# Turning the fourth tile of attention weights by DMA, with one normalization for a pair of heads

## The chip, the cores and the metric

The kernel runs on one NeuronCore of a Trainium2 chip. The metric is the device time of one execution in microseconds. TensorE (PE) multiplies into PSUM, VectorE (DVE) and ScalarE (ACT) read PSUM, GpSimd (POOL) works from SBUF alone, and SyncE (SP) issues all the DMAs of the loop. Each engine works its own instructions off in the order in which they were written, and waits on semaphores for the others.

## The reference

The program is a transformer block with adaptive layer norms: attention over the last 512 cached keys, then a gated MLP. The change touches the attention alone.

```python
h = _layernorm(x) * (1 + ca) + sa
q = (h @ wq).reshape(B, Sq, 32, 128).transpose(0, 2, 1, 3)       # Sq = 2048, x has 576 columns
k, v = (repeat(c[:, :, Sk - 512:, :], 2, axis=1) for c in (k_cache, v_cache))  # 16 heads of keys and values, each used twice
p = softmax(einsum("bhqd,bhkd->bhqk", q, k) * 128 ** -0.5)
o = einsum("bhqk,bhkd->bhqd", p, v)
x = x + ga * (o.transpose(0, 2, 1, 3).reshape(B, Sq, 32 * 128) @ wo)
...                                                               # second norm, then the MLP
```

## The kernel before

Nearly every product is made in float16 halves: a float32 operand is split in a high half (a cast) and a low half (the operand less its high half), and three matmuls (high by high, high by low, low by high) stand for one.

The attention is a list of 128 *slots*. A slot `i` is one query head with one block of 512 queries; slots come in pairs, an even slot with head j = 0 and an odd one with j = 1, both of the same key head and the same block. In a slot there are four *steps* t = 0 to 3, one for each tile of 128 queries. The main loop writes the work of one step down for all engines, and that written order is the order on every engine; no scheduler moves anything. Work of several slots is interleaved. In slot `i`:

- Step t: `scores(i, t)` makes the 128x512 scores (three matmuls into a bank `pss`, L400), DVE finds the row's maximum (L404) and turns it into the exponent's bias (L405), and `weights(i, t)` is the exponential on ACT with the row's sum beside it (L417, into `p` and column t of `l`).
- Tiles 0, 1 and 2: ACT casts `p` to its high half (`half_high`, L449), POOL makes the low half (`half_low`, L454), and two steps later SP issues a transposing DMA of both halves (`turn_away`, L461) into `ptw`, the weights with the keys on the partitions. The buffers `hp` that hold both halves are four (HF = 4).
- Tile 3: one slot on, at step 1, PE turns the float32 tile with four transposes into a bank of its own (`turn`, L440, a pool "T" of two banks), ACT casts it into `ptw` (`turn_high`, L444), DVE makes the low half (`turn_low`, L469, step 2).
- Steps 0 to 2: `query(i + 1, t)` makes the queries of the next slot in a bank `pq`; ACT copies the high half out at step 2 (L384), and `query_low(i + 1)` on DVE makes the low half at step 3 (L390).
- At the slot's end `values(i - 1)` multiplies `ptw` by the values: 12 matmuls into a bank `po` (L479). `pq` and `po` take turns in the two banks of the tag "A".
- `sums`: DVE inverts the row sums of slot i - 1 (L424), SP writes the 128x4 numbers to memory (`row`, L427) and reads them back spread over all partitions (`r`, L430, 256 KB). `normalize(i - 2)` at step 1 multiplies `po` by `r` (DVE, L488), and `split_on(i - 2)` at step 3 makes both halves `o` of the result (ACT L498, POOL L499).
- `attend_out`: each step has six matmuls of 288 columns (L353) that multiply `o` of an earlier pair by `wo`, into one bank pair `pe`, and after the second head DVE adds the result, times a factor, to the residual `acc` (L507).

Between these the loop holds side work in fixed places (weights of the MLP are split and stored, L679 to L738; keys and values are prepared). The MLP follows from slot 127 on.

## Time and profile before

| | us |
|---|---|
| median of three runs (2784.73 to 2787.59) | 2786.5 |
| the profiled execution | 2786.65 |
| its span, first to last instruction | 2784.8 |
| PE busy | 2707.0 (97%) |
| DVE busy | 2002.7 (72%) |
| POOL busy | 1864.4 (67%) |
| ACT busy | 1624.1 (58%) |

The span is the time between the first and the last instruction; what lies around it is 1.85 us here. Busy times are means over stages that differ: the attention ends near 1600 us, and DMA engines and POOL are far busier before that point than behind it. The matmuls' ends are modelled, so that successive matmuls overlap in the rows by some 0.16 us; the distance between two starts is the better measure of what a matmul takes.

### The profile page before, as it was taken

The numbers are of one execution on the slowest core, as the hardware profiler recorded it, in microseconds if no ns is written. First come the engines' busy times: TensorE is split into PE (matmuls) and PEld (weight loads), VectorE is DVE, ScalarE is ACT, GpSimd is POOL, SyncE is SP. The second block draws the span as 40 slices with busy tenths as digits, with TensorE's granted clock in tenths as the row PEclk, the third lists the DMA queues.
The fourth block names the chain that finished last, engine by engine and source line by source line (L and its number), as shares of the span: only waits on it lengthen the run. The fifth ranks groups of instructions, "written<-read, shape, count | busy, mean of one in ns | idle before, by whom it ended". The sixth has DMA issues, their size and how long they took to land.

```text
span 2784.8 us, 45011 instructions
## 1 busy us (share of the span) xinstructions
PE 2707.0 (97%) x15536; PEld 1535.3 (55%) x15536; DVE 2002.7 (72%) x3556; ACT 1624.1 (58%) x3022; POOL 1864.4 (67%) x1729
## 2 busy tenths in 40 slices
PE   6999999999999999999999999999999999999998
PEld 3455555555555555555555555555555555555555
DVE  7776788777788787887876657777766656566566
ACT  4686777777777877777677635544443333333332
POOL 3567788888788877777669637688774455333435
PEclk9999999999999999999999999999999999999999
DMA  5777888877777888878879945656643444333332
GB/s 162 177 168 187 189 186 185 179 178 187 169 181 172 187 200 186 212 181 205 194 185 220 233 125 169 195 165 199 206 152 103 160 123 127 104 102 112 105 110 77
DMA packets 594421, 463.27 MB, mean 166 GB/s; under 512 B 443152, under 2 KB 472976, under 8 KB 593424
## 3 DMA queue, kind: packets, MB, share of 16 engines
q1 hardware_dynamic: 593584, 460.39, 64.4%
q8 instruction: 122, 2.00, 0.3%
q14 instruction: 107, 0.88, 0.1%
q10 hardware_dynamic: 608, 0.00, 0.0%
HBM read 263.60 MB, written 95.99 MB: 129 GB/s over the span
## 4 chain that ended last, share of the span: by engine, by line
PE 50%; DVE 3%; DMA 1%; POOL 1%; issue 1%; ACT 0%; SPq 0%; DVEq 0%; POOLq 0%; ACTq 0%
PE py L764 15%; PE px L764 11%; PE pe L849 7%; PE pf L849 6%; PE pe L353 3%; PE po L479 2%; PE pss L400 2%; PE pq L342 2%; DMA row<-l 1%; DMA r<-row 0%; PE pt L440 0%; DVE acc L507 0%; DVE table L404 0%; PE pq L346 0%; POOL hp L454 0%
## 5 line engine op out<-in xcount | busy, mean ns | idle before, releaser
L454 POOL TENSOR_TENSOR hp<-p,hp 128x512 f16<-128x512 f32 x384 | 447.9, 1169 | 285.3 <-ACT hp L449 161.9
L417 ACT ACTIVATE p<-pss,table,factors 128x512 f32<-128x512 f32 x512 | 396.9, 775 | 362.0 <-DVE table L405 183.9
L764 PEld LDWEIGHTS <-wset 128*128 128x128 f16 x3528 | 345.7, 98 | 336.7 <-issue 4.0
L404 DVE TENSOR_REDUCE table<-pss 128x1 f32<-128x512 f32 x512 | 350.5, 685 | 211.8 <-PE pss L400 210.7
L764 PE MATMUL py<-hset,wset 128*128 128x512 f16 x2016 | 483.6, 380 | 0.0
L353 PE MATMUL pe<-o 128*128 128x288 f16 x3072 | 458.8, 286 | 14.6 <-DVE acc L507 12.5
L400 PE MATMUL pss<-k,qT 128*128 128x512 f16 x1536 | 417.3, 380 | 11.2 <-ACT p L417 9.2
L353 PEld LDWEIGHTS <-o 128*128 128x128 f16 x3072 | 300.4, 98 | 187.8 <-issue 20.9
L479 PE MATMUL po<-ptw,v 128*128 128x512 f16 x1536 | 358.2, 381 | 7.4 <-DVE ptw L469 5.6
L764 PE MATMUL px<-hset,wset 128*128 128x512 f16 x1512 | 361.5, 379 | 1.6 <-ACT p L417 1.6
L342 PE MATMUL pq<-hT,wq 128*128 128x512 f16 x1092 | 281.3, 380 | 1.1 <-DVE hT L211 1.1
L91 POOL TENSOR_TENSOR akv<-u,akv 128x512 f16<-128x512 f32 x141 | 164.8, 1178 | 174.6 <-ACT akv L90 166.8
L449 ACT CAST hp<-p 128x512 f16<-128x512 f32 x384 | 237.3, 618 | 12.9 <-POOL hT L213 0.4
L479 PEld LDWEIGHTS <-v 128*128 128x128 f16 x1536 | 150.9, 100 | 169.6 <-issue 16.8
L849 PEld LDWEIGHTS <-akv 128*128 128x128 f16 x1728 | 169.6, 98 | 93.6 <-issue 4.5
L400 PEld LDWEIGHTS <-qT 128*128 128x128 f16 x1536 | 150.4, 100 | 123.5 <-issue 12.6
L507 DVE SCALAR_TENSOR_TENSOR acc<-pe,factors,acc 128x576 f32<-128x576 f32 x256 | 207.7, 812 | 13.7 <-PE pe L353 10.4
L499 POOL TENSOR_TENSOR o<-on,o 128x512 f16<-128x512 f32 x128 | 150.2, 1173 | 55.8 <-ACT o L498 52.4
L342 PEld LDWEIGHTS <-wq 128*128 128x128 f16 x1104 | 108.6, 98 | 138.4 <-issue 9.0
L843 DVE SCALAR_TENSOR_TENSOR acc<-pf,table,acc 128x576 f32<-128x576 f32 x140 | 113.5, 811 | 80.6 <-PE pf L849 80.6
L944 ACT COPY u<-py 128x512 f32<-128x512 f32 x72 | 42.2, 586 | 200.5 <-PE py L764 198.6
L937 ACT ACTIVATE s<-s,table 128x512 f32<-128x512 f32 x72 | 52.0, 722 | 173.0 <-DVE s L936 173.0
(228 smaller groups left out, 4826.4 us busy)
## 6 DMA issues: line engine op xcount, KB each, us to landing
wset<-wd SPq DMA_DIRECT2D x213, 320.0 KB, 3.2
r<-row SPq DMA_DIRECT2D x128, 256.0 KB, 4.0
oset<-od SPq DMA_DIRECT2D x106, 288.0 KB, 3.2
wraw<-in_w SPq DMA_DIRECT2D x36, 768.0 KB, 5.5
wd<-wmade SPq DMA_DIRECT2D x75, 320.0 KB, 3.2
wset<-wd SPq DMA_DIRECT2D x71, 160.0 KB, 2.2
w2raw<-in_w SPq DMA_DIRECT2D x19, 576.0 KB, 4.9
wd<-ring SPq DMA_DIRECT2D x33, 320.0 KB, 2.8
```

Source lines behind the costliest of these rows:

```text
L91: eng.tensor_sub(halves[:, 1], src, halves[:, 0])
L342: nc.tensor.matmul(ps, w[:, k // 2, m, :], hT[:, DC + m if k == 1 else m, :], start=s == 0, stop=False)
L353: nc.tensor.matmul(E[:, h, :HALF], o[:, x, rows], w[:, y, h * HALF : (h + 1) * HALF], start=first and n == 0, stop=last and n == 2,)
L400: nc.tensor.matmul(pss, q[:, x, rows], k[:, y, :], start=n == 0, stop=n == 2)
L404: nc.vector.tensor_reduce(nm[:, 0:1], pss, axis=AX.X, op=ALU.max, negate=True)
L417: nc.scalar.activation(p, pss, AF.Exp, bias=nm[:, 1:2], scale=factor, accum_out=st["l"][:, t : t + 1])
L449: nc.scalar.copy(hp[:, 0, :], state[i]["p", t])
L454: nc.gpsimd.tensor_sub(hp[:, 1, :], state[i].pop(("p", t)), hp[:, 0, :])
L479: nc.tensor.matmul(po, v[:, x, c, :], pt[:, y, c, :], start=c == 0 and n == 0, stop=c == KC - 1 and n == 2)
L507: nc.vector.scalar_tensor_tensor(a, E[:, :, :HALF], factors[:, uses[u][0], 2:3], a, op0=ALU.mult, op1=ALU.add)
L764: nc.tensor.matmul(ps, w[:, a, :], h[:, b, :], start=start and n == 0, stop=stop and n == 6, skip_group_check=True)
L849: nc.tensor.matmul(ps[:, h, :HALF], a[:, rows], w[:, b, :], start=m == 0, stop=m == 2)
```

## The change

- All four tiles are split in SBUF (`half_high`, `half_low`) and turned by DMA; `turn`, `turn_high` and `turn_low` are gone. `turn_away` of tiles 2 and 3 stands at steps 0 and 1 of the following slot.
- The two "T" banks, which PE's transposes used, take the scores of tiles 0 and 2, so that scores have four banks.
- The even slot's head is not normalized. `normalize` and `split_on` bring `po` times 2^-24 straight into its halves: the high half on ACT at step 1, the low half on DVE at step 3, which reads `po` once more. The odd slot's head is multiplied by the ratio of both sums, and the inverse of the first head's sum goes into the factor with which `attend_out` adds to the residual. The sums of a pair lie in one tile `l`, and `sums` inverts, writes `row` and reads `r` once for a pair.

In the order of the instructions this shows at three places. All are from slot 60 (an even one) on; the names of tiles carry running numbers, and the line numbers differ a little between the programs (L404 is L405 in the changed one, L390 is L391, L479 is L468, L461 is L455).

PE at the end of slot 60, before: the last matmuls of `attend_out`, a small matmul of side work, then `values(59)`.

```order
L353 LDWEIGHTS o_8939
L353 MATMUL pe_76<-o_8802,o_8939 128x288
L1077 MATMUL pe_76<-table_217,ones_93 128x1 [waits DVE_49]
L479 LDWEIGHTS v_8356 [waits DMAHW5_49,DMAHW3_49,DMAHW1_49]
L479 MATMUL po_9103<-ptw_8893,v_8356 128x512 [waits Activation_49]
L479 LDWEIGHTS v_8356
L479 MATMUL po_9103<-ptw_8893,v_8356 128x512
L479 LDWEIGHTS v_8356
L479 MATMUL po_9103<-ptw_8893,v_8356 128x512 [waits DVE_49]
```

The same place now:

```order
L354 LDWEIGHTS o_8585
L354 MATMUL pe_76<-o_8456,o_8585 128x288
L1081 MATMUL pe_76<-table_217,ones_93 128x1 [waits DVE_49]
L468 LDWEIGHTS v_8024 [waits DMAHW3_49,DMAHW5_49,DMAHW2_49,DMAHW0_49]
L468 MATMUL po_8745<-ptw_8538,v_8024 128x512 [waits DVE_49]
L468 LDWEIGHTS v_8024
L468 MATMUL po_8745<-ptw_8538,v_8024 128x512
```

The first matmul of `values` waited for an ACT count and the third for the low half on DVE of the tile that PE had turned; now the group waits for four DMAs and, at its first matmul, for a count of DVE. In the built program that count is the one of `query_low` (L391, below): the tile `po` takes the bank of "A" that was given back first, and that is now the one of `pq`, since the even slot's `po` is read until step 3. This holds in 63 slots, all the even ones from 2 to 126; in the odd ones `po` takes the bank that `normalize` gave back at step 1, as before.

DVE in slot 60, from step 1 to step 3, before:

```order
L488 TENSOR_TENSOR on_9012<-po_8958,r_8927 128x512 [waits DMAHW0_49,Pool_49]
L507 SCALAR_TENSOR_TENSOR acc3_90<-pe_76,factors_95,acc3_90 128x576 [waits PE_49]
L241 TENSOR_REDUCE us_8952<-kvraw_8846 128x1 [waits DMAHW1_49]
L1072 TENSOR_REDUCE table_217<-w2raw_8925 128x1 [waits DMAHW7_49]
L404 TENSOR_REDUCE table_217<-pss_9040 128x1 [waits PE_49]
L405 TENSOR_SCALAR table_217<-table_217,factors_95 128x1 [waits DVE_49]
L469 TENSOR_TENSOR ptw_8893<-pt_9001,ptw_8893 128x4x128 [waits DMAHW3_49,Activation_49]
L404 TENSOR_REDUCE table_217<-pss_9071 128x1 [waits PE_49]
L405 TENSOR_SCALAR table_217<-table_217,factors_95 128x1 [waits DVE_49]
L390 SCALAR_TENSOR_TENSOR qT_9056<-pq_8985,qT_9056 128x512 [waits Activation_49]
L507 SCALAR_TENSOR_TENSOR acc0_87<-pe_76,factors_95,acc0_87 128x576 [waits PE_49]
```

And now:

```order
L511 SCALAR_TENSOR_TENSOR acc3_90<-pe_76,l_7800,acc3_90 128x576 [waits PE_49]
L242 TENSOR_REDUCE us_8598<-kvraw_8498 128x1 [waits DMAHW1_49]
L1076 TENSOR_REDUCE table_217<-w2raw_8569 128x1 [waits DMAHW7_49]
L405 TENSOR_REDUCE table_217<-pt_8682 128x1 [waits PE_49]
L406 TENSOR_SCALAR table_217<-table_217,factors_95 128x1 [waits DVE_49]
L405 TENSOR_REDUCE table_217<-pss_8712 128x1 [waits PE_49]
L406 TENSOR_SCALAR table_217<-table_217,factors_95 128x1 [waits DVE_49,Activation_49]
L391 SCALAR_TENSOR_TENSOR qT_8697<-pq_8632,qT_8697 128x512 [waits Activation_49]
L494 SCALAR_TENSOR_TENSOR o_8655<-po_8604,o_8655 128x512
L511 SCALAR_TENSOR_TENSOR acc0_87<-pe_76,l_8084,acc0_87 128x576 [waits PE_49]
```

`normalize` (L488) and `turn_low` (L469) have gone from the even slot; behind `query_low` stands the low half of the unnormalized head (L494), and `query_low` has kept its place behind the fourth maximum.

SP around the turns of slot 60, before:

```order
L461 DMA_TRANSPOSE ptw_9038<-hp_8981 128x8x128 [waits DMAHW6_49,PE_49,Pool_49]
L430 DMA r_9068<-row59_9020 128x512 [waits DMAHW7_49,DMAHW4_49]
L461 DMA_TRANSPOSE ptw_9038<-hp_9016 128x8x128 [waits DMAHW0_49,Pool_49]
L636 DMA wd14_118<-wmade_8997 128x640 [waits DMAHW1_49]
L461 DMA_TRANSPOSE ptw_9038<-hp_9049 128x8x128 [waits DMAHW2_49,Pool_49]
L427 DMA row60_9162<-l_8978 128x4 [waits DMAHW3_49,DVE_49]
L461 DMA_TRANSPOSE ptw_9182<-hp_9126 128x8x128 [waits PE_49,Pool_49]
```

And now:

```order
L455 DMA_TRANSPOSE ptw_8680<-hp_8627 128x8x128 [waits DMAHW6_49,PE_49,Pool_49]
L436 DMA r_8709<-row59_8662 128x512 [waits DMAHW7_49,DMAHW4_49]
L455 DMA_TRANSPOSE ptw_8680<-hp_8659 128x8x128 [waits DMAHW0_49,Pool_49]
L640 DMA wd14_118<-wmade_8644 128x640 [waits DMAHW1_49]
L455 DMA_TRANSPOSE ptw_8680<-hp_8690 128x8x128 [waits DMAHW2_49,Pool_49]
L455 DMA_TRANSPOSE ptw_8680<-hp_8721 128x8x128 [waits DMAHW3_49,Pool_49]
L455 DMA_TRANSPOSE ptw_8815<-hp_8767 128x8x128 [waits PE_49,Pool_49]
```

A slot has four transposes in place of three, and the even slot has no `row`; the odd one keeps `row` and `r`.

The diff (the removed functions and the main loop):

```diff
@ scores
-        pss = bank("S", "pss")
+        pss = bank("S", "pss") if t % 2 else t_bank()
@ weights
-            st["l"] = odd.tile([P, 2 * ST], F32, tag="l", name="l", bufs=3)
+            st["l"] = odd.tile([P, 6 * ST], F32, tag="l", name="l", bufs=4) if j == 0 else state[i - 1]["l"]
...
-        nc.scalar.activation(p, pss, AF.Exp, bias=nm[:, 1:2], scale=factor, accum_out=st["l"][:, t : t + 1])
+        nc.scalar.activation(p, pss, AF.Exp, bias=nm[:, 1:2], scale=factor, accum_out=st["l"][:, j * ST + t : j * ST + t + 1])
@ sums
+        if j == 0:
+            return
+        first, both, up, ratio = (st["l"][:, lo * ST : hi * ST] for lo, hi in ((0, 1), (0, 2), (2, 4), (4, 5)))
         if step == 0:
-            nc.vector.reciprocal(st["l"][:, ST:], st["l"][:, :ST])
+            nc.vector.reciprocal(up, both)
+            nc.vector.scalar_tensor_tensor(ratio, first, O_DOWN, up[:, ST:], op0=ALU.mult, op1=ALU.mult)
@ turn, turn_high, turn_low
-        for j in range(KC):
-            nc.tensor.transpose(ps[:, j, :], p[:, j * P : (j + 1) * P], ident)
-        nc.scalar.copy(st["pt"][:, 0, :, t * P : (t + 1) * P], st["t"])
-    nc.vector.tensor_sub(pt[:, 1, :, cols], state[i]["t"], pt[:, 0, :, cols])
@ normalize
+        if slots[i][1] == 0:
+            o = st["o"] = new_o(i)
+            nc.scalar.activation(o[:, 0, :], st["po"], AF.Copy, scale=O_DOWN)
+            return
@ split_on
+        if slots[i][1] == 0:
+            o, po = st["o"], st.pop("po")
+            nc.vector.scalar_tensor_tensor(o[:, 1, :], po, O_DOWN, o[:, 0, :], op0=ALU.mult, op1=ALU.subtract)
+            return
         on = st.pop("on")
+        nc.vector.tensor_scalar(
+            st["l"][:, 5 * ST :], st["l"][:, 2 * ST : 3 * ST], factors[:, uses[slots[i][0]][0], 2:3], 1.0 / O_DOWN,
+            op0=ALU.mult, op1=ALU.mult,
+        )
@ attend_out
-                a, E[:, :, :HALF], factors[:, uses[u][0], 2:3], a, op0=ALU.mult, op1=ALU.add
+                a, E[:, :, :HALF], state[2 * pair]["l"][:, 5 * ST + t : 5 * ST + t + 1], a, op0=ALU.mult, op1=ALU.add
@ main loop
-            if t == 0 and 1 <= i <= n:
-                turn_away(i - 1, 2)
-            slot, tile = (i - 1 if t == 1 else n, ST - 1)
-            if 0 <= slot < n:
-                turn(slot, tile)
+            if t < 2 and 1 <= i <= n:
+                turn_away(i - 1, t + 2)
...
-            if 1 <= i <= n and t == 2:
-                turn_low(i - 1, ST - 1)
...
-            if t < 3 and i < n:
+            if i < n:
                 half_high(i, t)
                 half_low(i, t)
-            if t == 1 and 1 <= i <= n:
-                turn_high(i - 1, ST - 1)
```

More of the change, by code (lines that the diff above doesn't have):

```diff
@@ L42 @@
 Q_DOWN = 2.0**-17
+O_DOWN = 2.0**-24
 EXPONENT = 0x7F800000
@@ L414, in weights @@
         if t == 0:
-            st["l"] = odd.tile([P, 2 * ST], F32, tag="l", name="l", bufs=3)
+            st["l"] = odd.tile([P, 6 * ST], F32, tag="l", name="l", bufs=4) if j == 0 else state[i - 1]["l"]
         p = pool.tile([P, SB], F32, tag="p", name="p", bufs=PB)
-        nc.scalar.activation(p, pss, AF.Exp, bias=nm[:, 1:2], scale=factor, accum_out=st["l"][:, t : t + 1])
+        nc.scalar.activation(p, pss, AF.Exp, bias=nm[:, 1:2], scale=factor, accum_out=st["l"][:, j * ST + t : j * ST + t + 1])
         st["p", t] = p
     def sums(i, step):
+        u, j, b = slots[i]
         st = state[i]
+        if j == 0:
+            return
+        first, both, up, ratio = (st["l"][:, lo * ST : hi * ST] for lo, hi in ((0, 1), (0, 2), (2, 4), (4, 5)))
         if step == 0:
-            nc.vector.reciprocal(st["l"][:, ST:], st["l"][:, :ST])
+            nc.vector.reciprocal(up, both)
+            nc.vector.scalar_tensor_tensor(ratio, first, O_DOWN, up[:, ST:], op0=ALU.mult, op1=ALU.mult)
         elif step == 1:
             st["row"] = dram.tile([P, ST], F32, name=f"row{i}")
-            nc.sync.dma_start(st["row"], st["l"][:, ST:])
+            nc.sync.dma_start(st["row"], ratio)
         elif step == 2:
@@ L432, in sums @@
             )
-    def turn(i, t):
-        st = state[i]
-        p = st.pop(("p", t))
-        ps = st["t"] = t_bank().rearrange("p (j n) -> p j n", j=KC)
-        for j in range(KC):
-            nc.tensor.transpose(ps[:, j, :], p[:, j * P : (j + 1) * P], ident)
-    def turn_high(i, t):
-        st = state[i]
-        nc.scalar.copy(st["pt"][:, 0, :, t * P : (t + 1) * P], st["t"])
     def half_high(i, t):
@@ L464, in turn_away @@
         )
-    def turn_low(i, t):
-        cols = slice(t * P, (t + 1) * P)
-        pt = state[i]["pt"]
-        nc.vector.tensor_sub(pt[:, 1, :, cols], state[i]["t"], pt[:, 0, :, cols])
     def values(i):
@@ L482, in values, with new_o @@
         st["po"] = po
+    def new_o(i):
+        return pool.tile([P, 2, SB], F16, tag=("ah", "al")[i % 2], name="o", bufs=3)
     def normalize(i):
         st = state[i]
+        if slots[i][1] == 0:
+            o = st["o"] = new_o(i)
+            nc.scalar.activation(o[:, 0, :], st["po"], AF.Copy, scale=O_DOWN)
+            return
         po = st.pop("po")
@@ L495, in split_on @@
         st = state[i]
+        if slots[i][1] == 0:
+            o, po = st["o"], st.pop("po")
+            nc.vector.scalar_tensor_tensor(o[:, 1, :], po, O_DOWN, o[:, 0, :], op0=ALU.mult, op1=ALU.subtract)
+            return
         on = st.pop("on")
-        o = st["o"] = pool.tile([P, 2, SB], F16, tag=("ah", "al")[i % 2], name="o", bufs=3)
+        nc.vector.tensor_scalar(
+            st["l"][:, 5 * ST :], st["l"][:, 2 * ST : 3 * ST], factors[:, uses[slots[i][0]][0], 2:3], 1.0 / O_DOWN,
+            op0=ALU.mult, op1=ALU.mult,
+        )
+        o = st["o"] = new_o(i)
         nc.scalar.copy(o[:, 0, :], on)
```

## The prediction

> **What bounds the kernel now.** I read the shares of the page first, then the busy times of stretches of the span, then what PE waited for.

> ```profile
> PE 2707.0 (97%) x15536; PEld 1535.3 (55%) x15536; DVE 2002.7 (72%) x3556; ACT 1624.1 (58%) x3022; POOL 1864.4 (67%) x1729
> ```

> ```profile
> core 0: us, PE busy (x) PEld busy (x) DVE busy (x) ACT busy (x) POOL busy (x), PEclk, DMA share, GB/s
> 250.20:1017.30 767.10, 756.15 (x4353) 427.88 (x4352) 605.10 (x1210) 596.13 (x1154) 649.24 (x627) 1.00 0.79 182
> 1017.30:1476.80 459.50, 455.78 (x2653) 260.66 (x2652) 359.56 (x734) 341.08 (x664) 332.31 (x308) 1.00 0.84 197
> 2000.00:2100.00 100.00, 96.55 (x542) 53.65 (x541) 69.44 (x98) 42.18 (x72) 70.54 (x63) 0.97 0.47 154
> ```

> The first two stretches are 64 and 38 slots of the attention, about 12 us each; PE is busy for 98.6% and 99.2% of them. The third lies in the MLP, which the change leaves alone. What PE waits for in the attention (45 to 1600 us):

> ```profile
> PE pss L400 <- ACT p L417: 9.2, 10, 2.5
> PE pe L353 <- DVE acc L507: 7.6, 10, 1.7
> PE po L479 <- DVE ptw L469: 5.6, 8, 2.9
> PE po L479 <- DMA ptw<-hp: 1.0, 2, 0.6
> ```

> All its waits there come to some 36 us. So PE is the bound: a matmul removed is a gain of its full length, and any wait put in front of PE is a loss of its full length.

> **What the change removes from PE.** The four transposes of a slot, in slot 60:

> ```profile
> 780.44 0.60 PE L440 MATMUL pt<-ident,p 128*128 128x128 f32 x4
> 780.88 0.81 PE L400 MATMUL pss<-k,qT 128*128 128x512 f16 x3
> ```

> From start to start they take 0.44 us; 128 slots give **-56 us**. Of the waits above, that for `turn_low` (5.6) goes with it; that for a bank of scores (9.2) should go with four banks; and that for `acc` (7.6) should halve, since DVE loses work. I take **-19 us**, between 0 (new lateness elsewhere) and -36 (all of them).

> **What the change puts in front of PE.** In the 63 even slots the first matmul of `values` now waits for `query_low` on DVE. The trace has no such wait, but it has both times. The end of slot 60:

> ```profile
> 785.59 0.81 PE L400 MATMUL pss<-k,qT 128*128 128x512 f16 x3
> 786.17 0.67 DVE L404 TENSOR_REDUCE table<-pss 128x1 f32<-128x512 f32 x1
> 786.24 0.90 PE L353 MATMUL pe<-o 128*128 128x288 f16 x6
> 787.11 2.95 PE L479 MATMUL po<-ptw,v 128*128 128x512 f16 x12
> 787.60 0.68 DVE L404 TENSOR_REDUCE table<-pss 128x1 f32<-128x512 f32 x1
> 788.32 0.21 DVE L405 TENSOR_SCALAR table<-table,factors 128x1 f32<-128x1 f32 x1
> 788.61 0.59 ACT L384 ACTIVATE qT<-pq 128x512 f16<-128x512 f32 x1
> 789.23 0.69 DVE L390 SCALAR_TENSOR_TENSOR qT<-pq,qT 128x512 f16<-128x512 f32 x1 [0.70 <-ACT qT L384]
> 789.89 0.81 PE L400 MATMUL pss<-k,qT 128*128 128x512 f16 x3
> ```

> `values` starts at 787.11 and `query_low` ends at 789.92, 2.81 us later. Before, that was hidden: only the third matmul of the next scores needed it, and the 2.6 us of `values` lay between. Now `values` itself stands behind it, and PE has nothing else to do. The same pair of rows in the first of the 63 slots, in the one with the least distance, and in the last:

> ```profile
> 80.88 0.59 PE L479 MATMUL po<-ptw,v 128*128 128x512 f16 x2
> 83.57 0.69 DVE L390 SCALAR_TENSOR_TENSOR qT<-pq,qT 128x512 f16<-128x512 f32 x1 [0.70 <-ACT qT L384]
> 354.94 2.76 PE L479 MATMUL po<-ptw,v 128*128 128x512 f16 x12 [0.25 <-ACT qT L384]
> 354.96 0.69 DVE L390 SCALAR_TENSOR_TENSOR qT<-pq,qT 128x512 f16<-128x512 f32 x1
> 1583.94 2.75 PE L479 MATMUL po<-ptw,v 128*128 128x512 f16 x12
> 1584.36 0.69 DVE L390 SCALAR_TENSOR_TENSOR qT<-pq,qT 128x512 f16<-128x512 f32 x1
> ```

> The distances are 3.38, 0.71 and 1.11; over the 63 slots the mean is 1.87, and 0.06 for the signal comes on top. So the upper end, if DVE and ACT are as late as now, is 63 x 1.93 = 122 us. The lower end is a slot in which neither is late: the slot at 354.94 had already waited 0.25, so it stands for 0.71 + 0.25 + 0.06, about 1.0 us, and 63 us in all. Lateness shrinks in part, because the even slot's DVE loses `normalize` and `turn_low`:

> ```profile
> L488 DVE TENSOR_TENSOR on<-po,r 128x512 f32<-128x512 f32 x128 | 138.9, 1085 | 16.8 <-POOL o L499 8.4 <-DMA r<-row 6.1 <-PE po L479 1.8
> L469 DVE TENSOR_TENSOR ptw<-pt,ptw 128x512 f16<-128x512 f32 x128 | 87.6, 684 | 26.6 <-ACT ptw L444 25.5 <-DMA row<-l 0.4 <-issue 0.2
> DVE qT L390 <- ACT qT L384: 62.2, 82, 1.8
> ```

> The last row (DVE's waits, 70 to 1600 us) says that in 82 of 126 slots DVE stood waiting for ACT's copy, so it is mostly ACT that is late there. But ACT's copy follows the exponential of tile 2, which waits for DVE's third maximum, and that one stood behind L488. In slot 60 it began at 786.17, about 2 us after its scores; without L488 all of this comes 1.07 us earlier. In a slot such as the last, nothing is gained. I take half a microsecond on average: 1.4 us a slot, **+88 us**.

> **What moves between the other engines.**

> ```profile
> L454 POOL TENSOR_TENSOR hp<-p,hp 128x512 f16<-128x512 f32 x384 | 447.9, 1169 | 285.3 <-ACT hp L449 161.9 <-issue 79.3 <-DVE table L405 16.8
> L449 ACT CAST hp<-p 128x512 f16<-128x512 f32 x384 | 237.3, 618 | 12.9 <-POOL hT L213 0.4
> L444 ACT CAST ptw<-pt 128x512 f16<-128x512 f32 x128 | 74.1, 579 | 0.6 <-PE pt L440 0.6
> L498 ACT CAST o<-on 128x512 f16<-128x512 f32 x128 | 78.1, 610 | 7.1 <-DVE on L488 7.1
> L499 POOL TENSOR_TENSOR o<-on,o 128x512 f16<-128x512 f32 x128 | 150.2, 1173 | 55.8 <-ACT o L498 52.4
> L461 SPq DMA_TRANSPOSE ptw<-hp x384: 1231/1239/3839, 45.1 to 1602.2; - x192
> DMA to landing us min/median/max: 3.0/3.8/8.2
> r<-row SPq DMA_DIRECT2D x128, 256.0 KB, 4.0
> SPq L461 <- POOL hp L454: 201.9, 101, 7.4
> ```

> ACT: 128 casts at 0.618 for 128 at 0.579, and 64 copies of `o` at 0.6 taken from PSUM instead of SBUF: +5 us in 1500, nothing. DVE: -128 x 0.684, -64 x (1.085 - 0.69), some 0.2 us rows less and more: about -110 us, which PE sees only as above. POOL: +128 x 1.169 - 64 x 1.173 = +75 us, 0.58 us a slot; it is busy 649 of 767 us in the fuller stretch, 10.1 us a slot, and goes to 10.7 of about 12.2, 88%. SP: one more issue of 1.24 us a slot, and half of the `row` and `r` issues gone. DMA engines: a transpose moves 256 KB, as `r` does. Its price is bounded by 1.1 us of all engines (their 606 busy microseconds in that stretch by 139 MB) and by 1.8 (the shortest landing, 3.0, less the issue of 1.24); with half an `r` gone that is +0.55 to +1.25 us a slot, and the share goes from 0.79 to 0.84 to 0.89.

> None of these becomes the bound, but two chains get shorter slack. Tile 3 needs a cast, POOL and a transpose before `values` one slot later: 0.62 + 1.17 + 3.8 = 5.6 us without queues. From the exponential's end to `values` there are 9.4 in slot 60 (the row below), less 0.44, plus the new wait of 1.4. And with four tiles a slot in four `hp` buffers, ACT's cast of a tile waits until the same tile of the slot before has landed: 5.6 us plus queues against a whole slot of 12. SP already waits up to 7.4 us for POOL, so some turns will be late: I take one slot in eight by 1 us, **+15 us**, between 0 and one in four by 2 us, 64.

> ```profile
> 776.90 0.78 ACT L417 ACTIVATE p<-pss,table,factors 128x512 f32<-128x512 f32 x1
> ```

> [...]

> **Sum.** -56 - 19 + 88 + 15 = +28 us. The profiled execution took 2786.65 us (0.15 above the median of the runs shown), so 2815 us.

> **Rivals.**
> - *Faster: DVE comes early enough.* The point of balance is a new wait of (56 + 19 - 15) / 63 = 0.95 us a slot. At the lower end of 1.0 us, with no new lateness and all of PE's old waits gone, it is 2786.65 - 56 - 36 + 63 = 2758. For it: DVE loses 110 us. Against: 82 waits of DVE for ACT, whose work stays.
> - *The wait doesn't exist* (`values` still goes ahead of `query_low`): 2786.65 - 56 - 19 + 15 = 2727. Against it stands the order of the instructions.
> - *POOL or the DMA engines fall behind,* so that turns are late as a rule: the upper ends of both, +122 + 64 - 56 - 19, 2898. For it: POOL at 88%, DMA at 0.89. Against: PE's 1.0 us.
> - *The clock drops.* The row of 2000 to 2100 us shows 0.97, and PE waited once there, for 3.4 us; a wait of 2.9 us in the attention left the clock at 1.00. The 0.03 of 100 us that are missing there are 3 us, a clock halved for 6. If the new waits were over 3 us in every even slot (their mean is 1.87, the first one 3.38), 63 x 3 = 189 us come on top, 3004.

> ```profile
> PE pe L849 <- DVE sums L843: 3.4, 1, 3.4
> ```

> [...]

> **How the numbers follow.** The forecast, slower by 0 to 85 us, has 0.66; faster by an early DVE 0.17; no wait 0.03; POOL or DMA 0.12; the clock 0.02. A difference under 0.2% (5.6 us) can't be told from none. Between the forecast's lower edge and the first rival's upper one lies that band, 0.09 in all: 0.05 from the forecast and 0.04 from the rival. So slower 0.61 + 0.12 + 0.02 = 0.75, same 0.09, faster 0.13 + 0.03 = 0.16. The range goes from the lower end of the first rival, 2758, to 2878 (the upper new wait of 122 with 45 of lateness, less 56 and 19); below and above it lie the no-wait case, half of POOL's and the clock's, and the tails, under 2 in 10.

> **What would show it.** PE's waits after should name `po` and DVE's `qT` (L391) 60 times or so, 60 to 120 us in all, about 1.4 us each, and no longer `ptw` from DVE. The distance of the scores' first matmul from the last matmul before it at step 1 shrinks by 0.44 us. Waits of PE for `ptw` from DMA should stay under 20 us, and waits of ACT's `hp` cast for a DMA be few. Even slots get longer by about 1 us, odd ones shorter by 0.5. The prediction is wrong if DVE's `qT` ends less than 0.9 us behind PE's arrival, or if `po` waits longer for DMAs than for DVE.

## The result, and the profile after

The changed kernel takes 2916.6 us (four runs, 2916.5 to 2916.9) against 2785.8 for the kernel before on the same chip (the three runs shown above and a fourth): 4.7% slower, ratio 1.0469 with a 95% interval of 1.0451 to 1.0487. The forecast was 2815, between 2758 and 2878. The direction was right; the size was not, and the time lies outside the range.

The engines' busy times, the two stretches that the prediction used, and PE's waits in the attention (45 to 1740 us; in total, times, longest):

```profile
PE 2704.9 (93%) x15024; PEld 1490.5 (51%) x15024; DVE 1964.0 (67%) x3492; ACT 1639.3 (56%) x3022; POOL 1936.6 (66%) x1793
```

```profile
core 0: us, PE busy (x) PEld busy (x) DVE busy (x) ACT busy (x) POOL busy (x), PEclk, DMA share, GB/s
250.20:1017.30 767.10, 696.22 (x3764) 373.44 (x3764) 538.33 (x1081) 549.73 (x1051) 621.91 (x599) 0.96 0.78 177
1017.30:1476.80 459.50, 416.67 (x2278) 224.91 (x2277) 325.90 (x664) 328.16 (x631) 352.37 (x323) 0.97 0.82 190
```

```profile
PE po L468 <- DVE qT L391: 128.2, 60, 5.5
PE po L468 <- DMA row<-l: 10.2, 2, 6.0
PE po L468 <- DMA ptw<-hp: 8.5, 3, 4.4
PE pe L354 <- DVE acc L511: 2.2, 2, 1.3
```

PE was busy for 98.6% of the first stretch before and is busy for 90.8% of it now, and its clock, 1.00 before, is 0.96. The wait that the prediction named is there, in 60 of its 63 slots, but at 2.14 us each and not 1.4. The end of slot 60, which the prediction showed for the kernel before:

```profile
846.82 0.81 PE L401 MATMUL pt<-k,qT 128*128 128x512 f16 x3
847.02 0.82 DVE L511 SCALAR_TENSOR_TENSOR acc<-pe,l,acc 128x576 f32<-128x576 f32 x1 [0.87 <-PE pe L354]
849.07 0.81 PE L401 MATMUL pss<-k,qT 128*128 128x512 f16 x3
849.61 0.68 DVE L405 TENSOR_REDUCE table<-pt 128x1 f32<-128x512 f32 x1
850.45 0.28 PE L1081 MATMUL pe<-table,ones 128*128 128x1 f32 x2
852.06 0.59 ACT L385 ACTIVATE qT<-pq 128x512 f16<-128x512 f32 x1
852.68 0.69 DVE L391 SCALAR_TENSOR_TENSOR qT<-pq,qT 128x512 f16<-128x512 f32 x1 [1.22 <-ACT qT L385]
853.43 4.41 PE L468 MATMUL po<-ptw,v 128*128 128x512 f16 x12 [2.70 <-DVE qT L391]
857.67 0.81 PE L401 MATMUL pt<-k,qT 128*128 128x512 f16 x3
```

PE ends its small matmul at 850.73 and stands until 853.43. Then the twelve matmuls of `values` take 4.41 us, where the row of before had 2.95: PE's clock is halved. The same moments by windows of 3.41 us, with the granted clock in the third column from the right:

```profile
846.57:849.98 3.41, 3.41 (x23) 1.98 (x21) 2.96 (x4) 2.00 (x4) 2.28 (x4) 1.00 1.19 221
849.99:853.40 3.41, 0.74 (x8) 0.60 (x6) 2.04 (x6) 2.73 (x6) 1.16 (x1) 1.00 1.09 187
853.41:856.81 3.40, 3.38 (x9) 1.14 (x9) 2.45 (x7) 2.95 (x6) 3.18 (x4) 0.50 0.43 87
```

One wait is paid twice: 2.70 us of standing, and some 1.5 us of slow matmuls behind it.

### The profile page after: what moved, and what is told of

Its sections match the earlier page's. It is cut to its first block, busy times and chain, and to the rows that moved or that the text cites. A ratio compares the mean times of both kernels' runs of the same rounds, so it can differ in the third digit from the quotient of the medians.

```text
span 2914.7 us, 44120 instructions
## 1 busy us (share of the span) xinstructions
PE 2704.9 (93%) x15024; PEld 1490.5 (51%) x15024; DVE 1964.0 (67%) x3492; ACT 1639.3 (56%) x3022; POOL 1936.6 (66%) x1793
## 3 DMA queue, kind: packets, MB, share of 16 engines
q8 instruction: 118, 1.93, 0.3%
## 4 chain that ended last, share of the span: by engine, by line
PE 51%; DVE 5%; ACT 3%; issue 2%; POOL 1%; DMA 1%; SPq 0%; ACTq 0%; DVEq 0%; POOLq 0%
PE py L768 15%; PE px L768 11%; PE pe L853 6%; PE pf L853 6%; PE po L468 4%; PE pe L354 3%; PE pq L343 2%; PE pt L401 1%; PE pss L401 1%; DVE table L405 1%; ACT p L418 1%; ACT hp L443 1%; DVE acc L511 1%; DVE qT L391 1%; ACT qT L385 0%
## 5 line engine op out<-in xcount | busy, mean ns | idle before, releaser
L448 POOL TENSOR_TENSOR hp<-p,hp 128x512 f16<-128x512 f32 x512 | 598.3, 1172 | 387.8 <-ACT hp L443 218.0
L468 PE MATMUL po<-ptw,v 128*128 128x512 f16 x1536 | 402.0, 417 | 151.4 <-DVE qT L391 128.2
L418 ACT ACTIVATE p<-pt,table,factors 128x512 f32<-128x512 f32 x256 | 198.5, 775 | 416.5 <-DVE table L406 374.1
L468 PEld LDWEIGHTS <-v 128*128 128x128 f16 x1536 | 161.6, 107 | 352.1 <-issue 208.0
L443 ACT CAST hp<-p 128x512 f16<-128x512 f32 x512 | 316.3, 618 | 26.4 <-DMA ptw<-hp 9.4
L405 DVE TENSOR_REDUCE table<-pss 128x1 f32<-128x512 f32 x256 | 176.0, 688 | 180.4 <-PE pss L401 180.2
L405 DVE TENSOR_REDUCE table<-pt 128x1 f32<-128x512 f32 x256 | 174.6, 682 | 156.3 <-PE pt L401 156.2
L511 DVE SCALAR_TENSOR_TENSOR acc<-pe,l,acc 128x576 f32<-128x576 f32 x256 | 207.7, 811 | 43.9 <-PE pe L354 35.3
L418 ACT ACTIVATE p<-pss,table,factors 128x512 f32<-128x512 f32 x256 | 197.8, 773 | 47.3 <-DVE table L406 45.3
L401 PE MATMUL pt<-k,qT 128*128 128x512 f16 x768 | 212.1, 385 | 6.4 <-ACT qT L385 4.3
L401 PE MATMUL pss<-k,qT 128*128 128x512 f16 x768 | 208.9, 381 | 0.0
## 6 DMA issues: line engine op xcount, KB each, us to landing
r<-row SPq DMA_DIRECT2D x64, 256.0 KB, 4.1
```

The source lines that it names most:

```text
L401: nc.tensor.matmul(pss, q[:, x, rows], k[:, y, :], start=n == 0, stop=n == 2)
L405: nc.vector.tensor_reduce(nm[:, 0:1], pss, axis=AX.X, op=ALU.max, negate=True)
L418: nc.scalar.activation(p, pss, AF.Exp, bias=nm[:, 1:2], scale=factor, accum_out=st["l"][:, j * ST + t : j * ST + t + 1])
L443: nc.scalar.copy(hp[:, 0, :], state[i]["p", t])
L448: nc.gpsimd.tensor_sub(hp[:, 1, :], state[i].pop(("p", t)), hp[:, 0, :])
L468: nc.tensor.matmul(po, v[:, x, c, :], pt[:, y, c, :], start=c == 0 and n == 0, stop=c == KC - 1 and n == 2)
```

## Accounts of every kernel

For each profiled execution I added up from its trace, over the attention (first matmul of the scores to the last of `values`): its length, PE's idle time between matmuls (gaps over 0.05 us), and the length of the stretches with a halved clock. A stretch at half clock costs half its length (within one group of 512-column matmuls, a start follows the one before it by a median of 0.427 us in the halved stretches of the changed kernel's trace and 0.216 outside them), and the removed transposes are worth 56 us. So the length should be 1582.2 (before) + change in idle time + half the change in halved time - 56 where the transposes are gone. Halved stretches are counted where they begin in the attention. The rows come from several chips, on which the kernel before took 2785.8 to 2788.6 us; each ratio is to the kernel before on the same chip, and differences of a few microseconds between rows mean little.

| kernel | time, us | ratio to before (95%) | attention | idle | halved | by the sum |
|---|---|---|---|---|---|---|
| before | 2785.8 | | 1582 | 43 | 10 | |
| changed | 2916.6 | 1.0469 (1.0451-1.0487) | 1713 | 174 | 133 | 1719 |
| 1 early split | 2813.0 | 1.0089 (1.0073-1.0106) | 1610 | 108 | 38 | 1605 |
| 2 pair's normalization alone | 2921.5 | 1.0481 (1.0464-1.0499) | 1712 | 147 | 58 | 1711 |
| 3 DMA turns alone | 2857.7 | 1.0251 (1.0235-1.0266) | 1658 | 144 | 61 | 1654 |
| 4 filled wait | 2891.0 | 1.0371 (1.0355-1.0388) | 1693 | 112 | 68 | 1692 |
| 5 early split, two score banks | 2810.8 | 1.0091 (1.0076-1.0106) | 1609 | 103 | 44 | 1604 |
| 6 early split, DVE half | 2807.4 | 1.0080 (1.0059-1.0100) | 1607 | 101 | 55 | 1607 |
| 7 DMA turns alone, DVE half | 2845.0 | 1.0212 (1.0197-1.0227) | 1644 | 129 | 68 | 1642 |
| 8 normalization alone, early split | 2804.0 | 1.0066 (1.0051-1.0081) | 1601 | 58 | 14 | 1600 |
| 9 early split, column parts | 2785.6 | 0.9994 (0.9984-1.0003) | 1579 | 81 | 17 | 1569 |
| 10 normalization alone, copied | 2840.1 | 1.0190 (1.0175-1.0206) | 1638 | 80 | 24 | 1626 |
| 11 changed, copied, column parts | 2895.1 | 1.0390 (1.0374-1.0405) | 1690 | 162 | 68 | 1675 |
| 12 as 8, more POOL work | 2821.0 | 1.0125 (1.0108-1.0142) | 1616 | 70 | 17 | 1613 |
| 13 changed, product's own bank | 2813.2 | 1.0094 (1.0077-1.0112) | 1611 | 105 | 48 | 1607 |
| 14 as 13, column parts | 2788.3 | 1.0003 (0.9994-1.0013) | 1587 | 86 | 27 | 1578 |
| 15 as 14, DVE half | 2789.9 | 1.0012 (1.0002-1.0021) | 1591 | 84 | 31 | 1578 |
| 16 DMA turns alone, own bank, column parts | 2839.3 | 1.0190 (1.0175-1.0206) | 1636 | 122 | 51 | 1627 |
| 17 as 14, a third score bank | 2816.9 | 1.0115 (1.0102-1.0129) | 1614 | 105 | 48 | 1607 |
| 18 as 17, DVE half | 2809.7 | 1.0090 (1.0076-1.0104) | 1609 | 97 | 51 | 1601 |

(In kernel 4 the added matmuls, 315 of some 0.215 us, are counted in.) The account closes within 6 us for the changed kernel and for ten of the others. The seven with column parts lie 7 to 15 us above it; they issue twelve more matmuls a slot, and in their traces the group of `values` takes 2.62 us from its start to the next matmul's, 2.59 in one part, which is 4 us of it. Kernel 10 lies 12 above; 8 us of that are matmuls of the query projection that take longer from start to start, and why stays open. So nearly all of what these edits did to the time is PE's idle time and the clock that follows it, with the 56 us of the transposes as forecast (in the trace of before all 512 of them take 55.9 us, from start to next start).

## The experiments

My theory (A) was the prediction's mechanism, larger: the even slot's product `po` takes the PSUM bank of `pq`, and so `values` waits for `query_low`. The rivals: the clock does most of the harm; the DMA turns themselves are late; POOL is behind.

**1. Release the bank a step earlier.**

```diff
-            if 2 <= i <= n and t == 3:
+            if 2 <= i <= n and t == (3 if slots[i - 2][1] else 2):
                 split_on(i - 2)
```

> The changed kernel with one line moved: the even head's low half (split_on on DVE) stands at step 2 instead of step 3, so that its bank of po is given back before that of pq, and values in the even slots no longer stands behind query_low. Theory A (the loss is the new wait of values for query_low, and the clock that drops behind it): PE's waits for po from DVE's qT, 128 us in the changed kernel, go to under 15 us, the TensorE clock over the attention is back at 0.99 or more, and the time is 2786 - 56 (the turns) - 5 to 20, that is 2710 to 2740 us. Rival B (turning four tiles by DMA overloads POOL and the DMA engines, and the wait for qT is only where it shows): the wait moves to ptw from DMA or to hp, and the time stays over 2850 us.

2813.0 us: 104 us of the 131 are gone, but not all, and the gain that A expected did not come. What PE waits for now:

```profile
PE po L468 <- DMA ptw<-hp: 42.7, 28, 4.7
PE po L468 <- issue: 10.9, 5, 3.0
PE po L468 <- DVE qT L391: 2.2, 1, 2.2
```

The wait for `query_low` has gone from 128.2 us to 2.2. Behind it stood another, for late turns, which it had covered: 35 times `values` waited for a turn, each time for that of tile 3. In those slots its issue ended 7.7 us after the next slot's first scores, in the others 4.7; from the start of the issue to the landing it took 4.3 and 3.8 us. So it is mostly the issue that is late, not the transfer.

**2. The pair's normalization alone** (tile 3 still turned by PE, two score banks, as before).

> The kernel before with the normalization of pairs alone (PE still turns the fourth tile, scores in two banks). Theory A: the order of the release of banks is the same as in the changed kernel, so the 63 waits of values for query_low are there, some 1.9 us each, 120 us in all, and the clock drops behind the longer ones: 2900 to 2970 us. Rival B: nothing is turned by DMA that was not before, so the time is that of before, 2770 to 2800 us.

2921.5 us. As A expected: no DMA turn of tile 3 is needed for the damage.

```profile
PE po L485 <- DVE qT L391: 114.1, 62, 3.1
```

**3. The DMA turns alone** (each head normalized by itself, four tiles by DMA, four score banks).

> The changed kernel without the normalization of pairs: four tiles split in SBUF and turned by DMA, scores in four banks, every head normalized as before (128 r and row transfers, 128 subtractions of o on POOL). Theory A: no wait for query_low, the turns' 56 us are gained: 2710 to 2745 us, though POOL and the DMA engines carry more than in the changed kernel. Rival B: POOL and the DMA engines are the bound, so it is as slow as the changed kernel or slower, over 2880 us.

2857.7 us, between both expectations. A missed: without the wait for `query_low`, turning by DMA still costs 70 us where it should give 56. PE waits in two places, for turns (the row "issue" is a wait for which the trace shows no releaser), and at the output projection for DVE's add; DVE in turn stands at `normalize` for a buffer that POOL releases late (last row, DVE's waits):

```profile
PE pe L354 <- DVE acc L494: 40.4, 26, 3.4
PE po L463 <- DMA ptw<-hp: 25.2, 20, 2.8
PE po L463 <- issue: 20.0, 12, 3.0
DVE on L475 <- POOL o L486: 30.6, 17, 3.7
```

So 2 and 3 don't add: +133 and +69 apart, +131 together. The turns' waits lie in the same place as that for `query_low`, which covers them, and the wait for DVE's add, 40.4 us here, is 2.2 with the pair's normalization.

**4. Fill the wait** with five matmuls of 512 columns that nobody reads, ahead of `values` in even slots of the changed kernel.

> The changed kernel with five more 512-column matmuls (1.08 us, into a free bank of scores, read by nobody) ahead of values in each even slot, in the time in which PE waits for query_low. Clock theory (part of theory A: the gaps halve the clock, 26 times and 116 us in the changed kernel's attention, which costs about half of that): PE's idle time falls by up to 68 us without the wait ending earlier, the clock drops less than 12 times, and the time falls by 25 to 55 us, to 2860 to 2892 us, although PE does more. If the clock costs nothing: the filler is hidden in the wait or adds to it, 2915 to 2940 us.

2891.0 us: more work on PE, and 26 us less time. The halved stretches fall from 133 to 68 us (16 of them, where fewer than 12 were expected), and the clock of the first stretch rises from 0.96 to 0.99. The clock's share is real, and it is a consequence of idle time.

```profile
250.20:1017.30 767.10, 727.42 (x4007) 392.32 (x4007) 551.96 (x1109) 566.15 (x1081) 637.25 (x615) 0.99 0.81 179
```

**5. Two score banks** in kernel 1, in place of four (`pss = bank("S", "pss")` for all tiles).

> The 2813.0-us run's kernel with the scores in two PSUM banks as before, not four. If four banks are what lets scores run ahead of late maxima and weights: over 2840 us. If PE's order, not the banks, sets the scores' start: 2800-2825 us, the same as with four.

2810.8, the same as kernel 1. Four banks weren't needed; two PSUM banks were free for something else, which 13 uses.

**6 and 7. The low half of tile 3 on DVE,** behind the next slot's first maximum, in kernels 1 and 3.

```diff
-        nc.gpsimd.tensor_sub(hp[:, 1, :], state[i].pop(("p", t)), hp[:, 0, :])
+        (nc.vector if t == 3 else nc.gpsimd).tensor_sub(hp[:, 1, :], state[i].pop(("p", t)), hp[:, 0, :])
...
-                half_low(i, t)
+                if t < 3:
+                    half_low(i, t)
+            if 1 <= i <= n and t == 0:
+                half_low(i - 1, 3)
```

> The changed kernel with the first head's low half taken one step earlier (as in the run at 2813.0 us), and with the low half of the fourth tile of weights made by DVE, behind the first maximum of the next slot, instead of by POOL. Theory P (POOL is behind): in the 2813.0-us run the turn of tile 3 was issued on average 4.1 us (even) and 3.9 us (odd) after the next slot's start, up to 10.3 us, while `values` starts without a wait only if it is issued by about 5.4 us; the cast had ended at 0.3 us, so the lateness is POOL's queue. On DVE the half ends at 2 to 3 us in every slot: PE's idle time before `values` falls from 75 us to under 30 us, and the time to 2735-2775 us. Theory D (the transfers themselves: DMA engines at 0.88 busy): the turn still lands late, idle time stays over 55 us, 2795-2820 us. Theory V (DVE pays): 128 more operations of about 0.6 us on DVE push back maxima and query halves, 2820 us or more.

> Turning all four tiles by DMA without the pair's normalization (the 2857.7-us run), with the low half of the fourth tile on DVE instead of POOL. Theory P: PE's idle time before `values` falls from 65 us to under 25, that before the output projection (which waits for DVE's add, and DVE for a buffer that POOL's late subtraction releases) from 47 us to under 20, and the time to 2745-2800 us. Theory D: 2835-2865 us. Theory V: over 2865 us.

2807.4 and 2845.0: 6 us better, which is within the noise (ratios 1.0080 and 1.0089), and 13, where theory P expected at least 38 and 58. P as I had put it (the last tile's own half is what is late) missed. Both times lie where theory D had them, but its reason, slow transfers, is the smaller part: where `values` waits for tile 3's turn, the issue ends 2.6 and 2.7 us later than in the other slots, and the landing takes 1.0 us longer. Kernel 7 in slot 23 shows how the issue comes to be late:

```profile
347.74 1.16 POOL L673 TENSOR_TENSOR wmade<-wraw,wmade 128x512 f16<-128x512 f32 x1
347.80 6.08 SPq L450 DMA_TRANSPOSE ptw<-hp  x2
348.97 1.00 POOL L674 TENSOR_TENSOR wmade<-wraw,wmade 64x256 f16<-64x256 f32 x1
349.16 0.62 ACT L438 CAST hp<-p 128x512 f16<-128x512 f32 x1
350.05 1.00 POOL L676 TENSOR_TENSOR wraw<-wraw 128x384 f32<-128x384 f32 x1
351.01 1.60 POOL L443 TENSOR_TENSOR hp<-p,hp 128x512 f16<-128x512 f32 x1
354.59 1.29 SPq L450 DMA_TRANSPOSE ptw<-hp  x1
```

Tile 3's half had been ready on DVE since 351.6 us. Its turn, the last row, was issued at 354.59, since SP issues in order, and the turn of tile 2 stood ahead of it for POOL, which was busy with the MLP's weights until 351.01. Taking one tile off POOL doesn't help when the tile ahead of it is still queued there.

**8. Kernel 2 with the early split.**

> The kernel before with the pair's normalization alone (the 2921.5-us run), and the first head's low half taken at step 2 instead of step 3. If the harm of the pair's normalization was only that PSUM bank, held until step 3, which `values` of every second slot then waits for: 2765-2795 us, as before within 0.4%, and no row of PE waiting for query_low over 15 us. If the pair's normalization costs in another way too (ACT's copy of the product, the late ratio): over 2830 us.

2804.0, between both expectations: the cure of kernel 1 takes 117 us off here too, which makes A's part independent of the turns. 18 us above before remain: `values` now waits for the split itself (DVE's `o`, 18.2 us, 23 times).

**9. Column parts** in kernel 1: tile 3 is a quarter of the product's columns, so it can come last.

```diff
-        for c in range(KC):
+        for part in (slice(0, 3 * P), slice(3 * P, SB)):
+          for c in range(KC):
...
-                    po, v[:, x, c, :], pt[:, y, c, :], ...
+                    po[:, part], v[:, x, c, :], pt[:, y, c, part], ...
```

> The 2813.0-us kernel (changed kernel, first head's low half a step earlier) with `values` taken in two column parts: first the twelve products of tiles 0 to 2 (384 columns), then the twelve of tile 3 (128 columns), so that tile 3's turn is needed some 3.4 us later (12 x 0.285 us). Theory L (only the last tile's turn is late, by up to 4 us): PE's idle time before `values` falls from 75 us to under 30 us; 2745-2790 us. Theory D (the turns of earlier tiles are late too, because SP and POOL are in order): idle stays over 50 us, 2800-2830 us. Theory O (twelve short products a slot cost more than they save, being bound by weight loads of 0.098 us): 2830 us or more.

2785.6, level with before. PE's idle time ahead of `values` fell from 75 to 29 us: theory L. (The 3.4 us of my expectation were worked from the rows' durations, which overlap; from start to start twelve whole products take some 2.6 us, so the tile got about 2.)

```profile
PE po L469 <- DMA ptw<-hp: 19.7, 16, 2.9
```

**10 and 11. Copy the first head's product out of PSUM at step 1,** by DVE, and split it from SBUF; alone with the normalization (10), and in the changed kernel with column parts (11).

> The kernel before with the pair's normalization alone, but with the first head's product copied out of its PSUM bank by DVE at step 1, where `normalize` stood, and split from SBUF later (ACT copy, DVE subtraction). Theory A (the bank held longer is all that the pair's normalization costs): 2765-2790 us, equal to or below before's 2786, with no wait for the first head's split (18 us at step 2) and none for query_low. Rival (the pair's normalization has a second cost, the late ratio or DVE's operations): 2800-2815 us, as with the split at step 2.

> The changed kernel with both cures: the first head's product copied out of PSUM at step 1, and `values` in two column parts so that tile 3's turn may come 3.4 us later. If the bank and the late turn of tile 3 are the whole cost that the change added: 2700-2765 us, below before. If turns of other tiles or DVE's extra work hold it: 2785-2830 us.

2840.1 and 2895.1: above every expectation, by a fault of the cure. No wait for `query_low` is left. But at step 3 DVE's subtraction stands directly behind ACT's copy, so DVE waits (second row of each pair, DVE's waits), and with it the add that frees the output projection's bank:

```profile
PE pe L354 <- DVE acc L530: 34.5, 38, 2.5
DVE o L513 <- ACT o L512: 72.1, 63, 2.1
```

```profile
PE pe L354 <- DVE acc L515: 94.4, 71, 5.5
DVE o L498 <- ACT o L497: 116.8, 63, 3.3
```

**12. More POOL work** in kernel 8: tile 0's low half twice.

> The 2804.0-us kernel (pair's normalization alone, split at step 2, fourth tile turned by PE) with POOL's low half of tile 0 computed twice in every slot: 128 more operations of 1.17 us on POOL, as many as the fourth tile's low half adds. If POOL's load costs only where a turn on the last tile waits for it: 2800-2812 us. If POOL's load by itself is what costs (about 25 to 70 us in the kernels with four DMA turns): 2825 us or more.

2821.0, 17 us more, between both expectations. POOL's load costs something by itself where PE turns tile 3. Turning tile 3 by DMA costs more: kernel 1 stands 6 us above kernel 8 (ratios 1.0089 and 1.0066), although it saves the 56 us of the transposes, so some 60.

**13. The product in a bank of its own.** Kernels 1 and 8 had also moved DVE's work; this moves none.

```diff
-        pss = bank("S", "pss") if t % 2 else t_bank()
+        pss = bank("S", "pss")
...
-        po = bank("A", "po")
+        po = t_bank()
```

> The changed kernel with one thing altered: the product `po` of `values` takes one of the two PSUM banks of the former turns, and the scores are all in their own two (two score banks cost nothing in the 2810.8-us run). The first head's low half stays at step 3. Theory A (PE waits for query_low only because the product's bank is the one that the query projection still holds): PE's wait for query_low falls from 128 us to under 10 us, the clock's share to 0.985 or more, 2795-2825 us. Rival (query_low and ACT are simply late in even slots, whatever the banks: scores of the next slot wait instead): 2870 us or more, with the idle time moved to the line of the scores.

2813.2, within A's range and 103 us below the changed kernel. The wait for `query_low` is gone altogether (the product is called `pt` here, by its new pool):

```profile
PE pt L468 <- DMA ptw<-hp: 36.8, 27, 5.5
PE pss L401 <- ACT p L418: 27.3, 26, 2.6
PE pt L468 <- issue: 12.0, 6, 3.2
```

That settles the first cause: which bank `po` takes was worth 103 us. `query_low` still ended 1.86 us after PE's arrival (the end of its last matmul ahead of `values`) on average over the even slots, 2.13 in the changed kernel; nothing needed to wait for it there.

**14, 15 and 16. Column parts on top** (14), tile 3's half on DVE as well (15), and the same bank and parts without the pair's normalization (16).

> The same, and `values` in two column parts, the fourth tile's last. Theory L (the late turn of the fourth tile is the rest): -25 to -45 us against the run with the product's own bank, 2755-2790 us. If landing times or earlier turns hold it: less than -10.

> The same again, and the fourth tile's low half on DVE behind the next slot's first maximum. If POOL's queue is what still delays turns: a further -10 to -25 us, 2740-2775 us. If DVE's maxima pay for it: 0 to +15.

> No pair normalization (the 2857.7-us kernel, all four tiles turned by DMA), with the product's own bank and `values` in two column parts. Theory L: PE's idle time before `values` falls from 65 to under 20 us, 2790-2825 us; what is left above the kernel before is the wait of the output projection (47 us), where POOL's subtractions hold the buffers that DVE's normalization needs. If turns are not the reason for the 65 us: 2840-2860 us.

2788.3, 2789.9 and 2839.3. The parts are worth 25 us again, and parts and bank together 18 without the normalization, where idle time ahead of `values` fell from 65 to 23 us. DVE's half gives nothing now (2 us, within the noise). In 14 what PE waits for is spread:

```profile
PE pss L401 <- ACT p L418: 34.5, 30, 3.8
PE pt L469 <- DMA ptw<-hp: 15.7, 11, 3.5
PE pe L354 <- DVE acc L513: 8.3, 10, 1.9
```

Kernel 16 came out at 2839 and not 2790 to 2825: it keeps a wait of 48 us at the output projection. That wait is one thing that the pair's normalization does cure: it halves POOL's subtractions of `o`.

**17 and 18. A third bank for the scores** in 14 and 15: tile 2's scores in the pool of the product.

> The 2788.3-us kernel (product in its own bank, columns of the fourth tile last), and the scores of tile 2 in the bank pair that the product uses, so that scores rotate over more than two banks. If the 38 us of PE's idle time ahead of the scores was a wait for a bank: it falls below 15 us, 2755-2778 us, below before by 0.3 to 1%. If ACT, which frees the banks, is itself late: the idle time moves to `values` and to the output projection, 2780-2795 us.

> The same, and the fourth tile's low half on DVE. If POOL's queue delays turns that PE then waits for (16 us of its idle time in the 2788.3-us kernel's trace): -5 to -15 us against the run above. If DVE's add behind it, for which the output projection waits (8 us there, 20 us with the low half on DVE), pays as much: within 5 us of it.

2816.9 and 2809.7: 29 and 20 us worse, and 17 outside both its expectations (18 stands 7 us below 17, as expected for POOL's queue). In 17 the idle time ahead of the scores fell from 38 to 18 us, as hoped, but ahead of `values` it rose from 22 to 49:

```profile
PE pt L469 <- ACT p L418: 31.3, 24, 3.7
```

The product, sharing a pool with a tile of scores, now takes a bank that ACT's exponential still reads. It is the first cause once more, made by my own hand. No version ran faster than the kernel before; 9 and 14 are level with it.

## Why the prediction was wrong

Its terms, and what the account gives for them in the changed kernel:

| term | predicted | found |
|---|---|---|
| transposes gone | -56 | -56 (they took 55.9; the account closes within 6 us in the eight kernels without them and without column parts) |
| PE's old waits | -19 | -13 (idle time not ahead of `values`, 35 to 22) |
| `values` for `query_low` | +88 | +128 |
| late turns | +15 | +16 (the rest of the idle time ahead of `values`, 7 to 23) |
| clock | 0 | +61 (halved time 10 to 133, half of it) |
| sum | +28 | +136; measured +131 |

The 5.6 us of the wait for `turn_low`, which are gone, lay ahead of `values`: put where the prediction had them, the second and fourth rows read -19 and some +21. The 103 us that the forecast was short are two rows: the clock, put at nothing, 61, and the wait for `query_low`, 40.

- **The mechanism and its place were right**: the row is `po` for DVE's `qT`, 60 times; the scores' wait for ACT and the wait for DVE's low half are gone. From one slot's first scores to the next one's, even slots take 14.63 us (12.13 before) and odd ones 11.80 (12.23): the odd ones' half microsecond is as forecast, the even ones grew by 2.5 and not by 1.
- **"I take half a microsecond on average: 1.4 us a slot"** failed; it was 2.14, above even the upper end of 1.93. `query_low`, which was to end earlier, ended 2.13 us after PE's arrival on average over the 63 slots, 1.74 before: it ends 0.28 us later, counted from the third scores' start, and PE arrives 0.11 earlier. The half microsecond was to come from `normalize` leaving DVE's queue ahead of the third maximum. DVE before and after, the stretch between the second and third maximum of slot 60:

```profile
782.59 1.07 DVE L488 TENSOR_TENSOR on<-po,r 128x512 f32<-128x512 f32 x1
783.59 0.80 DVE L507 SCALAR_TENSOR_TENSOR acc<-pe,factors,acc 128x576 f32<-128x576 f32 x1
786.17 0.67 DVE L404 TENSOR_REDUCE table<-pss 128x1 f32<-128x512 f32 x1
```

```profile
847.02 0.82 DVE L511 SCALAR_TENSOR_TENSOR acc<-pe,l,acc 128x576 f32<-128x576 f32 x1 [0.87 <-PE pe L354]
847.76 0.68 DVE L242 TENSOR_REDUCE us<-kvraw 128x1 f32<-128x512 f32 x1
848.35 1.34 DVE L1076 TENSOR_REDUCE table<-w2raw 128x1 f32<-128x1152 f32 x1
849.61 0.68 DVE L405 TENSOR_REDUCE table<-pt 128x1 f32<-128x512 f32 x1
```

  Where `normalize` stood, DVE now waits 0.87 us for PE, because the add behind it needs PE's output projection of that step. The third maximum begins 2.79 us after its scores' start, 2.83 before; over the 63 slots it is 1.67 and 1.71. I removed an operation from a queue and didn't look at what the next one in it waits for.

  On top, ACT is later, which the prediction had put at "nothing": in the even slots its third exponential starts 0.70 us after its bias is ready, 0.39 before, and its copy for `query_low` starts 0.27 us later, counted from the third scores' start. What fits is the new copy of `po`, which stands ahead of the second exponential:

```profile
845.72 0.59 ACT L480 ACTIVATE o<-po 128x512 f16<-128x512 f32 x1
```

  The same lag is 0.66 to 0.81 us in the eleven kernels, the changed one among them, that have this copy at step 1 and tile 3's half not on DVE. It is less in the others: the three with that half on DVE (6, 15, 18) have 0.52 to 0.62, the four that keep `normalize` (before, 3, 7, 16) 0.31 to 0.43, and the two that copy on ACT at step 3 (10 and 11) 0.50 and 0.44. Kernels 1 and 13, whose odd slots are as long as before, have the longer lag too, so it isn't a backlog from shorter odd slots. No run moved this copy alone.
- **The clock's chance of 0.02** failed by its condition, "over 3 us in every even slot". Idle time well short of that halved the clock: 2.70 us in slot 60, and gaps of 1.6 and 1.8 us in kernel 3 (last section).
- **The late turns were right only by cover.** With the bank free (13), idle time ahead of `values` was still 57 us, 7 before. The prediction's rule for them, one slot in eight by 1 us, is what was seen while PE stood for `query_low` anyway. Late turns, as the POOL rival (0.12) had them, are what is left of this change without its main fault, though in 39 slots of 124 and not as a rule.
- So even without the bank, the change would not have gained: in 13, -56 for the transposes, +62 of idle time and +19 of clock give +25, and 13 stands 25 us above before (2813.2 to 2788.5).

## What to carry to other kernels

When an edit makes a PSUM buffer live longer, follow which bank each later tile of that pool takes: here one bank choice put `values` behind an unrelated operation and cost 103 us, and giving the product another pool took it all back. When an operation is removed from an in-order queue, ask what the next one waits for before counting the time as won. And price a wait in front of PE with the clock behind it: add what stands in the same window, since in these traces 129 of the 130 windows of 3.413 us with less than 40% of work were followed by half clock.

## What the hardware showed

```profile
L455 SPq DMA_TRANSPOSE ptw<-hp x512: 1231/1233/4708, 44.8 to 1736.0; - x171
```
